# Batch 0's q heads in two PSUM banks, masks from one 64-column tile, batch 1 loaded pair by pair, tile 0 in two chunks

## The chip, the cores and the metric

The kernel runs on one core of a Trainium2 chip. A core has five engines that run side by side: TensorE (PE in the profile; its weight loads are PEld), VectorE (DVE), ScalarE (ACT), GpSimd (POOL) and SyncE (SP), each with its own in-order queue of instructions, and 16 DMA engines that they share. TensorE writes to PSUM, which has eight banks[...]. The metric is the device time of one execution in microseconds (us).

## The reference

Attention with a causal window of 64 positions over 8 batches, 8 heads, 576 positions and a head size of 64, and behind it an MLP with SiLU on its 4608 rows.

```python
scores = scale * np.matmul(q, k.transpose(0, 1, 3, 2))       # q, k, v: (8, 8, 576, 64) float32
rel = pos[:, None] - pos[None, :]
mask = (rel >= 0) & (rel < 64)
scores = np.where(mask, scores, -1e9)
attn = softmax(scores)                                       # over the last axis
x = (attn @ v).transpose(0, 2, 1, 3).reshape(4608, 512)
h = x @ w_in                                                 # (512, 2048)
out = (h * sigmoid(h)) @ w_out                               # (2048, 512), float32
```

## The kernel before

**Order.** The program is not written in its final order. Every piece of work is an operation in a list (`p.add(class, {engine: us}, function, deps, ...)`), and when the kernel is built a planner (`Plan.run`) plays the lists through: each engine takes, of the classes whose first operation is ready by the plan's clock, the one of the lowest rank, and the operations are issued in the order in which they were taken. The `us` of an operation, the `dma` of a load and the terms in `Plan.run` (line 98) are the plan's own cost numbers. They set the order on each in-order queue, and do not appear on the chip in any other way. An engine waits on the chip when its next instruction isn't ready, whatever stands behind it.

**Attention.** Heads are worked in pairs (four pairs `pj` per batch) and query rows in three groups `g` of 192. For each pair, q and k come in rows (`natb`), TensorE turns them (line 299, or line 309 in batch 0, where the load casts to bf16 on the way), and the turned blocks are lifted from PSUM to SBUF: `lift_q` (line 316) writes each head of the pair to its own half of the partitions of `qbd`, the other half of which is zero, and `lift_k` (line 322) writes `kt`. In batch 0 both heads of q are turned into one bank, and the two lifts read this bank. v is loaded into every second block of `vv`, and `shift_v` (lines 330 and 332) copies the halves that the overlapping key blocks need. Scores (line 344; 351 and 356 in batch 0), exponential (line 362), mask, values (line 370), reciprocal (line 376), norm, turning back (line 426; 415 in batch 0) and the copy into `bridge` (line 431) follow for each pair and group. From batch 2 on k, and later q and the outputs, are turned by DMA instead.

**Mask.** In batch 0, where TensorE has time, the mask is added to the scores: a matmul of the identity with `bias` or `bias0` (line 351) opens each score bank. From batch 1 on the exponentials are multiplied by `mask` or `mask0` (line 365). GpSimd builds `bias` and `mask` over six repeats of 64 columns each (lines 182 to 185), `bias` between the loads of pairs 1 and 2 of batch 0, `mask` behind the loads of pair 3; VectorE copies them to `bias0` and `mask0` and closes one block there.

**Loads.** GpSimd's queue carries, in this order: the identity; batch 0's q, k, v pair by pair (lines 241 and 269), with `bias` among them; `mask`; w_in in eight pieces (line 275); batch 1's q and k of all four pairs (line 234); two zero fills of `qbd` for batch 1 (line 218); batch 1's v (line 269); w_out in eight pieces (line 281); batch 2 and so on. `NIV` is the number of batches whose v is loaded pair by pair with q and k.

**MLP.** Rows go in nine tiles of 512. The first layer of a tile (line 435) runs over 16 blocks of 128 hidden units with 4 matmuls each, every block followed by a SiLU on ScalarE (line 441); the second layer (line 444) over 16 blocks for each of four row blocks, then a copy (line 450) and a store (line 454). `PARTS` cuts the columns of a first layer into chunks that can start when their rows of `bridge` are there: three for tile 0, two for tile 1. MLP matmuls have the rank behind all attention work, so they fill what attention leaves of TensorE; `scores_may_run` holds score matmuls back in the middle of a first layer. For the beginning there are up to 60 filler matmuls (line 668).

Of the kernel before, what the change touches and what calls it, by code (L numbers as in the profile page):

```python
# [9 lines left out]
BF16 = mybir.dt.bfloat16  # L10
ACTF = mybir.ActivationFunctionType
ALU = mybir.AluOpType


class Plan:
# [31 lines left out]
    def run(self):  # L47
# [7 lines left out]
        while left:  # L55
# [6 lines left out]
            while moved:  # L62
                moved = False
                for e in engines:
# [28 lines left out]
                    if op["dma"] is None:  # L93
                        op["seen"] = end + op["lat"]
                    else:

                        soft = e == "POOL"
                        pipe[soft] = max(pipe[soft], pipe[False], end + 0.6) + op["dma"]
                        op["seen"] = pipe[soft] + (2.0 if c in ("xk", "xo") else 1.4)
# [11 lines left out]
def kernel(ctx, tc, q, k, v, w_in, w_out, out):  # L111
# [16 lines left out]
    PARTS = {0: [(0, 192), (192, 384), (384, TT)], 1: [(0, 256), (256, TT)]}  # L128
    NXQ, NXK, NXO = 4, 2, 3
    NRAW, NOX = 2, 2  # L130
    NIV, NPM = 1, 1
# [10 lines left out]
    zero = keep.tile([128, NP], FP32, name="zero")  # L142
    mask0 = keep.tile([128, 3, 2, 64], BF16, name="mask0")
# [36 lines left out]
    def windows(t, fill, in_):  # L180
        m2 = t.rearrange("p t h i -> p (t h) i")
        nc.gpsimd.memset(m2, in_)
        nc.gpsimd.affine_select(out=m2, in_=m2, compare_op=ALU.is_ge, fill=fill,
                                base=-1, channel_multiplier=1, pattern=[[0, 6], [-1, 64]])
        nc.gpsimd.affine_select(out=m2, in_=m2, compare_op=ALU.is_ge, fill=fill,
                                base=64, channel_multiplier=-1, pattern=[[0, 6], [1, 64]])

    def const_bias(_):
        windows(bias, -30000.0, 0.0)

    def const_bias0(_):
        nc.vector.tensor_copy(out=bias0, in_=bias)
        nc.vector.memset(bias0[0:64, 0], -30000.0)

    def const_mask(_):
        windows(mask, 0.0, 1.0)

    def const_mask0(_):
        nc.vector.tensor_copy(out=mask0, in_=mask)
        nc.vector.memset(mask0[0:64, 0], 0.0)  # L200
# [29 lines left out]
    c_bias, c_mask = [], []  # L230
# [73 lines left out]
    def turn_heads(op, w):  # L304
        pst = at_bf16(op).rearrange("x (m p) -> x m p", m=NM)
        heads = natbs[w].rearrange("p m x -> p (m x)").rearrange("p (h m d) -> p h m d", h=2, m=NM)
        for m in range(NM):
            for hh in range(2):
                nc.tensor.matmul(  # L309
                    pst[64 * hh:64 * hh + 64, m], lhsT=heads[:, hh, m], rhs=ident[0:NR, 0:NR],  # L310
                    is_transpose=True, start=(m == 0), stop=(m == NM - 1),
                )
# [166 lines left out]
    def add_batch_qk(b):  # L479
        pool = "at" if b else "all"  # L480
        slot, parts = {}, {0: [], 1: []}
        for pj in range(NP):
            kq_done[(b, pj)] = []
            busy = s_last.get((b - NK, pj), []) + ([c_k[b % NK]] if b < NK else [])
            if (b, pj) == (0, 2):
                b1 = p.add("dma", {"POOL": 1.5}, const_bias)
                c_bias.append(p.add("one", {"DVE": 0.4}, const_bias0, [b1]))
            for kk in range(2):
# [29 lines left out]
                if b == 0:  # L518
                    ca = [p.add("dma", {"POOL": 0.66}, lambda _, w=w, pj=pj, kk=kk: load_cast(w, pj, kk), dma=0.87)]
                else:  # L520
                    i = n_nat[0] % NN
                    n_nat[0] += 1
                    cls, us = ("dma", {"POOL": 0.85}) if b in (1, 2) else ("ld0", {"SP": 0.45})
                    ld = p.add(cls, us, lambda e, i=i, pj=pj, kk=kk: load_qk(e, i, b, pj, kk),
                               [nat_free.get(i)] + (v_landed[b - 1] if b > 2 else []), dma=1.1)
                    ca = [p.add("cast", {"ACT": 0.84, "DVE": 0.56}, lambda e, i=i, w=w: cast(e, i, w),
                                [ld, natb_free.get(w)], b=b)]
                    nat_free[i] = ca[0]
                tu = p.add("turn", {"PE": 0.27 if b else 0.7}, None, ca + [c_ident] + busy, lat=0.1, pool=pool, b=b)
                tu["fn"] = lambda _, tu=tu, w=w: (turn if b else turn_heads)(tu, w)  # L530
                natb_free[w] = tu
                by = {"ACT": 0.64, "DVE": 0.75}
                if kk:
                    li = [p.add("lift", by, lambda e, tu=tu, pj=pj: lift_k(e, tu, b, pj), [tu] + busy, b=b)]
                else:
                    li = [p.add("lift", by, lambda e, tu=tu, pj=pj, hh=hh: lift_q(e, tu, b, pj, hh), [tu] + busy, b=b)
                          for hh in range(2)]
                tu["until"] = li
# [4 lines left out]
    def add_v_loads(b, parts, busy):  # L543
        v_landed.setdefault(b, []).extend(
            p.add("dma", {"POOL": 1.0}, lambda e, part=part: load_v(e, b, part), busy, dma=1.25) for part in parts)
# [117 lines left out]
    c_mask1 = p.add("dma", {"POOL": 1.5}, const_mask)  # L663
    c_mask.append(p.add("late", {"DVE": 0.4}, const_mask0, [c_mask1]))
# [8 lines left out]
    for f in range(8):  # L673
        win.append(p.add("dma", {"POOL": 0.8}, lambda _, f=f: load_w_in(f), dma=1.45))
    add_batch_attention(0)
    n_tile = 0
    for b in range(1, B):
# [4 lines left out]
        if b == 1:  # L682
            for f in range(8):
                wout.append(p.add("dma", {"POOL": 0.8}, lambda _, f=f: load_w_out(f), dma=1.45))
# [38 lines left out]
```

## Time and profile before

| | |
|---|---|
| median of 6 runs | 324.61 us (323.27 to 328.06) |
| the profiled execution, own time | 324.87 us |
| its span, first to last instruction | 323.1 us |
| mean granted TensorE clock | 0.989 |
| busy: PE, PEld | 305.2 us, 177.3 us |
| busy: ACT, DVE, POOL | 193.5, 165.4, 122.0 us |
| DMA moved | 39.41 MB in 135775 packets |

The profile is of one execution. Its rows by slices cut the span into 40 parts of 8.1 us and give tenths: a digit of 9 is 90% or more. The clock row gives what TensorE was granted of its full clock. In a timeline a row has the start, the duration, the engine, the line of the kernel, the operation, what is written and read, and in brackets how long the engine had been idle and what ended the wait. A matmul's own duration includes its latency, so for a stream of them the distance from start to start is used.

### The profile page before, as it was taken

The numbers are of one execution on the slowest core, as the hardware profiler recorded it, in microseconds if no ns is written. First come the engines' busy times: TensorE is split into PE (matmuls) and PEld (weight loads), VectorE is DVE, ScalarE is ACT, GpSimd is POOL, SyncE is SP. The second block draws the span as 40 slices with busy tenths as digits, with TensorE's granted clock in tenths as the row PEclk, the third lists the DMA queues.
The fourth block names the chain that finished last, engine by engine and source line by source line (L and its number), as shares of the span: only waits on it lengthen the run. The fifth ranks groups of instructions, "written<-read, shape, count | busy, mean of one in ns | idle before, by whom it ended". The sixth has DMA issues, their size and how long they took to land.

```text
span 323.1 us, 6251 instructions
## 1 busy us (share of the span) xinstructions
PE 305.2 (94%) x2289; PEld 177.3 (55%) x2314; DVE 165.4 (51%) x471; ACT 193.5 (60%) x392; POOL 122.0 (38%) x162
## 2 busy tenths in 40 slices
PE   1979979999999999999999999999999999999996
PEld 1657966668766555554554455445544444444444
DVE  3874796882888899893389178904810000000000
ACT  6658894688877757457835683568257226415611
POOL 8976966947272985875357000000000000000000
PEclk9979997999999999999999999999999999999999
DMA  8999999999999999999999983400430020021012
GB/s 89 137 166 244 200 199 222 164 129 276 151 158 157 168 150 155 179 139 200 144 175 182 160 127 91 114 3 0 117 89 0 34 81 16 0 85 46 1 56 76
DMA packets 135775, 39.41 MB, mean 122 GB/s; under 512 B 121664, under 2 KB 130496, under 8 KB 135744
## 3 DMA queue, kind: packets, MB, share of 16 engines
q0 software_dynamic: 93760, 19.54, 73.9%
q1 hardware_dynamic: 41984, 19.47, 31.9%
q8 instruction: 18, 0.29, 0.4%
q14 instruction: 13, 0.11, 0.1%
HBM read 36.70 MB, written 9.44 MB: 143 GB/s over the span
## 4 chain that ended last, share of the span: by engine, by line
PE 81%; DMA 8%; POOL 5%; DVE 3%; issue 1%; SPq 0%; ACT 0%; POOLq 0%; ACTq 0%
PE mp L444 38%; PE mp L435 32%; PE at L370 5%; PE at L344 5%; DMA nat<-in_k_dram 3%; DMA nat<-in_q_dram 3%; DMA w_in_sb<-in_moe_w_in_dram 3%; POOL natb L241 2%; POOL vv L269 1%; POOL w_in_sb L275 1%; PE at L299 1%; DVE qbd L316 1%; PE at L426 1%; DVE natb L288 1%; DVE ot L450 1%
## 5 line engine op out<-in xcount | busy, mean ns | idle before, releaser
L444 PE MATMUL mp<-w_out_sb,g 128*128 128x512 bf16 (+2 forms) x583 | 143.0, 369 | 1.1
L435 PE MATMUL mp<-bridge,w_in_sb 128*128 128x512 bf16 (+3 forms) x768 | 130.4, 326 | 0.4 <-ACT g L441 0.4
L441 ACT ACTIVATE g<-mp 128x512 bf16<-128x512 f32 (+3 forms) x192 | 91.2, 492 | 30.3 <-PE mp L435 29.0
L435 PEld LDWEIGHTS <-w_in_sb 128*128 128x128 bf16 x768 | 69.6, 98 | 52.1 <-issue 0.8
L444 PEld LDWEIGHTS <-g 128*128 128x128 bf16 x608 | 55.3, 98 | 43.1 <-issue 0.6
L450 ACT COPY ot<-mp 128x512 f32<-128x512 f32 (+2 forms) x33 | 18.5, 561 | 69.5 <-PE mp L444 61.4
L362 ACT ACTIVATE e<-at 128x384 bf16<-128x384 f32 x90 | 39.3, 497 | 7.1 <-PE at L344 5.8
L399 DVE TENSOR_TENSOR ox<-at,rc 64x192 bf16<-64x192 f32 x120 | 42.3, 353 | 2.4
L251 POOL DMA_DIRECT2D nat<-in_k_dram x48 | 35.0, 734 | 17.9 <-DMA vv<-in_v_dram 7.7
L365 DVE TENSOR_TENSOR e<-e,mask 128x384 bf16<-128x384 bf16 x84 | 26.3, 347 | 23.5 <-ACT e L362 22.8
L269 POOL DMA_DIRECT2D vv<-in_v_dram x32 | 32.7, 1025 | 14.2 <-PE at L370 9.6
L370 PE MATMUL at<-vv,e 128*128 128x130 bf16 x270 | 29.9, 221 | 4.0 <-DVE e L365 2.1
L370 PEld LDWEIGHTS <-e 128*128 128x128 bf16 x288 | 23.3, 98 | 18.5 <-DVE e L365 4.5
L251 POOL DMA_DIRECT2D nat<-in_q_dram x32 | 24.0, 756 | 13.5 <-DMA vv<-in_v_dram 9.0
L344 PE MATMUL at<-qbd,kt 128*128 128x128 bf16 x252 | 23.4, 220 | 0.2
L344 PEld LDWEIGHTS <-kt 128*128 128x128 bf16 x252 | 18.1, 98 | 8.4 <-issue 1.1
L376 DVE RECIPROCAL rc<-at 128x6 f32<-128x6 f32 x90 | 17.4, 195 | 9.2 <-PE at L370 7.2
L316 DVE COPY qbd<-at 64x576 bf16<-64x576 bf16 x22 | 16.6, 755 | 8.3 <-ACT qbd L316 4.3
L382 DVE TENSOR_TENSOR ob<-at,rc 64x192 bf16<-64x192 f32 x48 | 16.7, 349 | 0.9
L265 DVE COPY qbd<-raw 64x1152 bf16<-64x1152 bf16 x16 | 9.1, 570 | 8.8 <-DMA raw<-nat 8.4
L431 ACT CAST bridge<-at 128x192 bf16<-128x192 f32 x22 | 7.1, 323 | 6.0 <-PE at L426 4.6
L309 PE MATMUL at<-ident,natb 96*64 96x96 bf16 x72 | 3.4, 246 | 7.4 <-DMA natb<-in_q_dram 7.4
(70 smaller groups left out, 170.9 us busy)
## 6 DMA issues: line engine op xcount, KB each, us to landing
out_dram<-ot SPq DMA_DIRECT2D x35, 256.0 KB, 2.7
vv<-in_v_dram POOLq DMA_DIRECT2D x32, 144.0 KB, 7.8
nat<-in_k_dram POOLq DMA_DIRECT2D x48, 72.0 KB, 6.8
nat<-in_q_dram POOLq DMA_DIRECT2D x8, 288.0 KB, 9.6
nat<-in_q_dram POOLq DMA_DIRECT2D x32, 72.0 KB, 7.6
w_in_sb<-in_moe_w_in_dram POOLq DMA_DIRECT2D x8, 256.0 KB, 7.5
w_out_sb<-in_moe_w_out_dram POOLq DMA_DIRECT2D x8, 256.0 KB, 8.6
nat<-in_k_dram POOLq DMA_DIRECT2D x4, 288.0 KB, 10.3
```

The costliest lines, as they stand in the source:

```text
L251: nc.gpsimd.dma_start(out=rows(i)[:, pj % 2, :, 64 * hh:64 * hh + 64], in_=(q, k)[kk][b, 2 * pj + hh].rearrange("(m p) d -> p m d", p=NR),)
L269: queue[e].dma_start(out=vv[b % NK][:, 2 * g0 + 1:2 * g1 + 1:2, 0:D], in_=v[b].rearrange("h s d -> (h s) d").rearrange("(g p) d -> p g d", ...
L316: copies[e](out=qbd[b % NK][r, pj, hh].rearrange("x (p m) -> x p m", m=NM), in_=at_bf16(op)[r].rearrange("x (m p) -> x p m", m=NM),)
L344: nc.tensor.matmul(at_sp(op)[:, x], lhsT=kt[b % NK][:, pj * S + t * 64:pj * S + t * 64 + 128], rhs=qbd[b % NK][:, pj, :, t * 64:t * 64 + 6 ...
L362: nc.scalar.activation(out=es[n % NE], in_=at_sp(op), func=ACTF.Exp, scale=scale)
L365: nc.vector.tensor_mul(es[n % NE], es[n % NE], mask0 if g == 0 else mask)
L370: nc.tensor.matmul(at_pv(op)[:, x], lhsT=es[n % NE][:, x].rearrange("p h i -> p (h i)"), rhs=vv[b % NK][:, s:s + NB + 1:NB, 0:D + 1], star ...
L399: nc.vector.tensor_mul(ox(n)[:, :, r], pv[r, :, hh, 0:D], rc[r, :, hh:hh + 1].to_broadcast([64, 3, 64]))
L435: nc.tensor.matmul(banks[bank["bank"]][:, lo:hi], lhsT=w_in_sb[:, c, ft * 128:(ft + 1) * 128], rhs=bridge[:, (j * TT + lo) // 64:(j * TT + ...
L441: nc.scalar.activation(out=gts[gt][:, lo:hi], in_=banks[bank["bank"]][:, lo:hi], func=ACTF.Silu)
L444: nc.tensor.matmul(banks[bank["bank"]][:, 0:hi - lo], lhsT=gts[gt][:, m * 128:(m + 1) * 128], rhs=w_out_sb[:, f, lo:hi], start=(f == 0), s ...
L450: copies[e](out=ots[ot][:, lo:hi], in_=banks[bank["bank"]][:, 0:hi - lo])
```

## The change

The identity's tile is followed on GpSimd by a `window` tile of 64 columns (a memset and two selects), ahead of all loads; VectorE spreads it into `bias` and `bias0` with broadcast copies, and later computes `mask` and `mask0` from these with a multiply and an add (-32768 becomes 0, 0 becomes 1). The two places in GpSimd's queue where `bias` and `mask` were built are gone. In batch 0, the heads of a q pair are turned as two operations, each with a bank and one lift of its own. `NIV` is 2, so batch 1 is loaded as q, k, v of each pair in turn, and its zero fills come behind these loads. Tile 0 has two chunks instead of three, tile 1 one instead of two. In the plan, a second lift from the same bank now waits for the first, and the cost numbers of the loads are changed. These numbers and the new dependencies can change the planned order throughout.

```diff
-                        pipe[soft] = max(pipe[soft], pipe[False], end + 0.6) + op["dma"]
+                        pipe[soft] = max(pipe[soft], pipe[False], end + 0.9) + op["dma"]
...
-    PARTS = {0: [(0, 192), (192, 384), (384, TT)], 1: [(0, 256), (256, TT)]}
+    PARTS = {0: [(0, 192), (192, TT)]}
...
-    NIV, NPM = 1, 1
+    NIV, NPM = 2, 1
...
+    window = keep.tile([128, 64], BF16, name="window")
...
-    def windows(t, fill, in_):
-        m2 = t.rearrange("p t h i -> p (t h) i")
-        nc.gpsimd.memset(m2, in_)
-        nc.gpsimd.affine_select(out=m2, in_=m2, compare_op=ALU.is_ge, fill=fill,
-                                base=-1, channel_multiplier=1, pattern=[[0, 6], [-1, 64]])
-        nc.gpsimd.affine_select(out=m2, in_=m2, compare_op=ALU.is_ge, fill=fill,
-                                base=64, channel_multiplier=-1, pattern=[[0, 6], [1, 64]])
+    def const_window(_):
+
+        nc.gpsimd.memset(window, 0.0)
+        nc.gpsimd.affine_select(out=window, in_=window, compare_op=ALU.is_ge, fill=-32768.0,
+                                base=-1, channel_multiplier=1, pattern=[[-1, 64]])
+        nc.gpsimd.affine_select(out=window, in_=window, compare_op=ALU.is_ge, fill=-32768.0,
+                                base=64, channel_multiplier=-1, pattern=[[1, 64]])
 
     def const_bias(_):
-        windows(bias, -30000.0, 0.0)
-
-    def const_bias0(_):
-        nc.vector.tensor_copy(out=bias0, in_=bias)
-        nc.vector.memset(bias0[0:64, 0], -30000.0)
+        for t in (bias, bias0):
+            nc.vector.tensor_copy(out=t.rearrange("p t h i -> p (t h) i"),
+                                  in_=window.unsqueeze(1).to_broadcast([128, 6, 64]))
+        nc.vector.memset(bias0[0:64, 0], -32768.0)
 
     def const_mask(_):
-        windows(mask, 0.0, 1.0)
-
-    def const_mask0(_):
-        nc.vector.tensor_copy(out=mask0, in_=mask)
-        nc.vector.memset(mask0[0:64, 0], 0.0)
+        for a, m in ((bias, mask), (bias0, mask0)):
+            nc.vector.tensor_scalar(m, a, 1.0 / 32768.0, 1.0, op0=ALU.mult, op1=ALU.add)
...
-    c_bias, c_mask = [], []
+    c_window = p.add("one", {"POOL": 0.6}, const_window)
+    c_bias = [p.add("one", {"DVE": 0.9}, const_bias, [c_window])]
+    c_mask = [p.add("late", {"DVE": 0.7}, const_mask, c_bias)]
...
-    def turn_heads(op, w):
+    def turn_heads(op, w, hs):
         pst = at_bf16(op).rearrange("x (m p) -> x m p", m=NM)
         heads = natbs[w].rearrange("p m x -> p (m x)").rearrange("p (h m d) -> p h m d", h=2, m=NM)
         for m in range(NM):
-            for hh in range(2):
+            for hh in hs:
...
-            if (b, pj) == (0, 2):
-                b1 = p.add("dma", {"POOL": 1.5}, const_bias)
-                c_bias.append(p.add("one", {"DVE": 0.4}, const_bias0, [b1]))
...
-                    ca = [p.add("dma", {"POOL": 0.66}, lambda _, w=w, pj=pj, kk=kk: load_cast(w, pj, kk), dma=0.87)]
+                    ca = [p.add("dma", {"POOL": 0.66}, lambda _, w=w, pj=pj, kk=kk: load_cast(w, pj, kk), dma=1.0)]
...
-                tu = p.add("turn", {"PE": 0.27 if b else 0.7}, None, ca + [c_ident] + busy, lat=0.1, pool=pool, b=b)
-                tu["fn"] = lambda _, tu=tu, w=w: (turn if b else turn_heads)(tu, w)
+                by = {"ACT": 0.64, "DVE": 0.75}
+                li = []
+
+                for hs in ([(0,), (1,)] if b == 0 and not kk else [(0, 1)]):
+                    us = 0.27 if b else 0.35 * len(hs)
+                    tu = p.add("turn", {"PE": us}, None, ca + [c_ident] + busy, lat=0.1, pool=pool, b=b)
+                    tu["fn"] = lambda _, tu=tu, w=w, hs=hs: turn(tu, w) if b else turn_heads(tu, w, hs)
+                    if kk:
+                        tu["until"] = [p.add("lift", by, lambda e, tu=tu, pj=pj: lift_k(e, tu, b, pj), [tu] + busy, b=b)]
+                    else:
+                        for hh in hs:
+                            tu["until"].append(p.add("lift", by, lambda e, tu=tu, pj=pj, hh=hh: lift_q(e, tu, b, pj, hh),
+                                                     [tu] + busy + tu["until"], b=b))
+                    li += tu["until"]
                 natb_free[w] = tu
...
-    c_mask1 = p.add("dma", {"POOL": 1.5}, const_mask)
-    c_mask.append(p.add("late", {"DVE": 0.4}, const_mask0, [c_mask1]))
```

Left out of the diff are the other changed cost numbers of loads: batch 1's q and k 1.1 to 1.15, v 1.25 to 1.3, w_in 1.45 to 1.55, w_out 1.45 to 1.38.

More of the change, by code (lines that the diff above doesn't have):

```diff
@@ L524, in add_batch_qk @@
                     ld = p.add(cls, us, lambda e, i=i, pj=pj, kk=kk: load_qk(e, i, b, pj, kk),
[L525 removed]
+                               [nat_free.get(i)] + (v_landed[b - 1] if b > 2 else []), dma=1.15)
                     ca = [p.add("cast", {"ACT": 0.84, "DVE": 0.56}, lambda e, i=i, w=w: cast(e, i, w),
@@ L528, in add_batch_qk @@
                     nat_free[i] = ca[0]
-                tu = p.add("turn", {"PE": 0.27 if b else 0.7}, None, ca + [c_ident] + busy, lat=0.1, pool=pool, b=b)
-                tu["fn"] = lambda _, tu=tu, w=w: (turn if b else turn_heads)(tu, w)
-                natb_free[w] = tu
[L532 to L538, printed above, removed]
+                by = {"ACT": 0.64, "DVE": 0.75}
[11 more added lines that the diff above has]
+                    li += tu["until"]
+                natb_free[w] = tu
                 kq_done[(b, pj)] += li
@@ L544, in add_v_loads @@
         v_landed.setdefault(b, []).extend(
-            p.add("dma", {"POOL": 1.0}, lambda e, part=part: load_v(e, b, part), busy, dma=1.25) for part in parts)
+            p.add("dma", {"POOL": 1.0}, lambda e, part=part: load_v(e, b, part), busy, dma=1.3) for part in parts)
     def add_batch_v(b):
@@ L673 @@
     for f in range(8):
-        win.append(p.add("dma", {"POOL": 0.8}, lambda _, f=f: load_w_in(f), dma=1.45))
+        win.append(p.add("dma", {"POOL": 0.8}, lambda _, f=f: load_w_in(f), dma=1.55))
     add_batch_attention(0)
@@ L683 @@
             for f in range(8):
-                wout.append(p.add("dma", {"POOL": 0.8}, lambda _, f=f: load_w_out(f), dma=1.45))
+                wout.append(p.add("dma", {"POOL": 0.8}, lambda _, f=f: load_w_out(f), dma=1.38))
         while TB * (n_tile + 1) <= b * NB:
```

## The prediction, made before the changed kernel was run

> **What bounds the kernel now.** I read the engine rows first, then the chain of work that ended last, then the landings of the DMAs, then the timelines of the two places where TensorE stands still.
>
> ```profile
> PE 305.2 (94%) x2289; PEld 177.3 (55%) x2314; DVE 165.4 (51%) x471; ACT 193.5 (60%) x392; POOL 122.0 (38%) x162
> PE   1979979999999999999999999999999999999996
> PEclk9979997999999999999999999999999999999999
> ```
>
> TensorE bounds the kernel from slice 7 on (a slice is 8.1 us). Everything that can still be won lies in the first 50 us and in the two dips of the clock row (slices 2 and 6). Behind them VectorE is done at 240 us and TensorE has only matmuls left, so a microsecond that tile 1 starts earlier is a microsecond of the end.
>
> ```profile
> 14.23 3.67 POOL w_in_sb L275 x5
> 17.90 8.38 DMA w_in_sb<-in_moe_w_in_dram
> 26.56 9.07 DMA nat<-in_k_dram
> 35.65 1.49 DVE natb L288 x2
> ```
>
> The chain runs through GpSimd's issues to 17.90, then through DMA to 35.65. The completion times in the trace say how tight that is: batch 0's twelve loads land from 4.81 (q of pair 0) to 17.17 (v of pair 3), one per 1.12 us; w_in from 19.16 to 29.18, one per 1.43; batch 1's q and k from 30.87 to 39.29 and its v to 42.91; w_out from 44.16 to 53.18, one per 1.29. The DMA row shows no hole between 3.3 and 53 us.
>
> ```profile
> 17.52 0.75 DVE L316 COPY qbd<-at 64x576 bf16<-64x576 bf16 x1
> 18.30 0.64 ACT L316 COPY qbd<-at 64x576 bf16<-64x576 bf16 x1 [1.57 <-DVE qbd L316]
> 18.96 0.49 ACT L362 ACTIVATE e<-at 128x384 bf16<-128x384 f32 x1
> 19.50 0.51 PE L370 MATMUL at<-vv,e 128*128 128x130 bf16 x3 [1.75 <-ACT e L362]
> ```
>
> And the same stretches in the table by windows (start:end, length, busy PE, PEld, DVE, ACT, POOL, clock, DMA share, GB/s):
>
> ```profile
> 20.00:25.00 5.00, 5.00 (x52) 3.80 (x50) 2.97 (x11) 3.35 (x10) 2.77 (x5) 0.73 1.39 182
> 45.00:50.00 5.00, 2.09 (x19) 1.16 (x19) 4.68 (x14) 3.14 (x5) 2.98 (x5) 1.00 1.24 206
> 50.00:55.00 5.00, 5.00 (x41) 3.14 (x40) 2.97 (x10) 2.53 (x7) 2.95 (x5) 0.66 1.51 230
> ```
>
> Stand-still one, in the timeline: ScalarE's half of a q pair waits 1.57 us for VectorE's half, because both read one bank; the exponential behind it is late, and TensorE waits 1.75 us and then runs at half clock. Stand-still two: of the 5 us from 45 TensorE works 2.09, while VectorE works 4.68. It is behind with batch 1's casts, lifts and eight v shifts; the mask runs at 48.59, though ScalarE began that score group at 46.19. The clock falls again (0.66).
>
> **Part by part.**
>
> *The window tile goes ahead of the first load.* A GpSimd select took 0.29 us on 128 columns and 0.54 on 384, a memset 0.20 and 0.44: a straight line gives 0.23 and 0.14 for 64. Two selects, a memset and three gaps of 0.07 come to 0.81 us, and every load of batch 0 is issued that much later. It removes 1.6 us of GpSimd before pair 2 (6.31 to 7.91) and 1.6 before w_in (12.53 to 14.18). I credit the first with nothing: q of pair 2 landed 0.72 us after the load ahead of it, so the DMA side was just in step, and the pace of 1.12 us holds before and after that hole. So q of pair 0 lands at 5.6, k of pair 3 at 17.05 instead of 16.25. If the deeper queue does speed the stream up, pair 3 lands at 15.5, the issue bound. I keep 17.05. The second hole is worth 0.6: the first w_in came 1.99 us after the last v, the others 1.43 apart. From w_in on the stream is therefore 0.2 us late: w_out begins at 44.4.
>
> *The masks on VectorE.* Two copies (0.26), a memset (0.17), and later two multiply-adds (about 0.26 each) replace a copy and memset of each kind (0.43 and 0.36): 0.4 us more of VectorE in all, the first part in idle time at 2 to 3 us. A rule speaks against it. The Trainium skill (SBUF — State Buffer, "Who interferes with whom") says that a VectorE copy in a two-port mode and GpSimd lock each other out for a whole instruction, and these copies run while GpSimd writes the first descriptors. The row: v shifts, copies within SBUF too, took 0.60 to 0.82 us beside GpSimd's issues instead of 0.32, while an issue beside such copies took 0.79 instead of 0.68. By the rule the first loads could wait both copies, 0.5 us; by the row 0.1. I take 0.1, which the w_in gap swallows.
>
> *Two banks for q.* The same 12 transposes, but head 0 is lifted while head 1 is turned, and neither engine waits for the other. VectorE waited for ScalarE's half 3.8 us in three places, ScalarE for VectorE's 1.6. Pair 0: q at 5.6, head 0 turned 0.35 later, lifted by 6.6; k at 6.4, turned by 7.1, lifted (0.64) by 7.8. The bias is long there, where it came only at 9.25. First scores at 7.9 instead of 9.46. Pair 3: k at 17.05, turn 0.45, lift 0.76: its scores begin at 18.3 instead of 21.08, since neither wait of stand-still one is left. From these scores to tile 0 it took 6.1 us (21.08 to 27.19): tile 0 starts near 24.4. Bank pressure: one more of eight for half a microsecond, nothing.
>
> *Tile 0 in two chunks, tile 1 in one.* Start to start a matmul of 128, 192, 256 and 512 columns takes 58, 83, 111 and 216 ns, so 320 takes 137. Tile 0's first layer: 64 x (83+83+58) = 14.3 us becomes 14.1. Tile 1: 128 x 111 = 14.2 becomes 13.8, 0.4 us less. Waiting for all of batch 0 costs nothing, its groups end together; for tile 1 see the rivals.
>
> *Tile 0's early start is mostly taken back.* At 24.4 the w_in pieces just keep ahead (the last lands at 29.4; TensorE asks at 28.9: 0.5 lost). The first layer ended 17.2 us after its start with six turns inside; now at about 41. The second layer cannot start before w_out lands, 44.4. So 2.8 us of start become 46.09 - 44.4 = 1.7.
>
> *Batch 1 pair by pair.* Same loads, but v of pair 0 lands at about 33.3 instead of 40.3, so the shifts (0.32 each) move into VectorE's idle stretch (30 to 35: 1.60 of 5 busy), and k of pair 3 lands at 42.1 instead of 39.3. That costs nothing while k waits anyway: its cast ran at 47.32. The two zero fills (2.46 us) move behind v on GpSimd, ahead of w_out: that is issued near 37.8, and landings of 7.4 us after issue hold 3 us of queue, so it still comes at 44.4. Stand-still two, 2.1 us (46.9 to 49.0), goes, because the three score groups that now run after 41 have 3 us without second-layer work.
>
> *The half clock.* TensorE then has little to do for some 3 us before 44.4. The Trainium skill (TensorE: Matmul & The Clock Gate, "HAM oscillation — how this bites in real kernels") puts the limit at idle gaps over about 3.4 us: scores in between would keep the clock, and 1.5 us more would be won. The rows are stricter: gaps of 1.75 and 2.1 us each brought about 3 us at 0.50 (from 19.3 and 50.0), losing 1.5. I leave the 1.5 lost.
>
> **The sum.** From the turn at 45.83 to tile 1's start at 69.97 TensorE has 64 x 0.216 = 13.8 us of second layer, 9 score groups x 0.17, 12 value groups x 0.17, 12 x 0.09 back, and six turns x 0.26: 20.0. Begun at 44.4, less 0.4 of turns done before, plus 1.5 half clock and 0.5 small waits: 66.0, so 4.0 gained. With tile 1's 0.4: 4.4. The profiled execution took 324.87 (span 323.1 and 1.8 around it), 0.3 over the median of 324.61. 324.87 - 4.4 = **320.5**.
>
> **Rivals.**
> *A, the start is won and then lost in batch 1.* VectorE does some 3.6 us per pair (a cast, two lifts, k's lift, two shifts) against a landing pace of 3.2, and it stood idle from 31.6 to 34.07 because a turn sat behind MoE matmuls in TensorE's order. If that stays, its backlog ends near 48 as before, stand-still two grows by the 1.7 won: only tile 1's 0.4 is left, 324.4. For it: VectorE at 4.8 of 5 from 35 to 50. Against: ScalarE is freed of 16 silus after 41.
> *B, pair 3 of batch 1 becomes the wait: slower.* The scores go group by group over all pairs, so every group needs pair 3, and tile 1 in one piece needs the last group. k is 2.8 us later, and VectorE, the bound in A, adds 1.6 of lag. The last bridge moves from about 68.3 to 72.7; tile 1 starts 2.7 later, the idle from 66 on costs 1.7 of clock: 324.87 + 2.7 + 1.7 - 0.4 = 328.9. It decides from the point where the last bridge is later than 70.4. Against it: 8 us of slack on k's cast.
> *That batch 0 gains nothing* (the 0.8 is all that is left) leads to A's number, since w_out sets the next start.
>
> **How the numbers follow.** Forecast 0.62, own range 317.5 to 322.5 (without the half clock 319.0, and with the deeper queue's 1.5 us 317.5); A 0.20; B 0.18. A measurement of this kernel tells about 1% from no change, 3.2 us: faster begins at 321.4. Nine tenths of the forecast lie below that: 0.57 faster; B's upper three quarters and a little more are slower, 0.16; the rest 0.27. The range reaches through A into B: 317.0 to 327.5.
>
> **What would show it.** First scores before 8.5; ScalarE's wait for VectorE's lift gone; tile 0 at 23.5 to 25.5; w_out from 44 to 45; second layer within 0.5 us of it; no 2 us gap after 46; tile 1 near 66. Wrong if pair 3 of batch 0 lands after 18.5, w_out after 46, or the last bridge of batch 1 after 70.

## The result, and the profile after

The changed kernel takes 323.18 us (median of 35 runs), the kernel before 325.63 (72 runs); the ratio is 0.9935, with a 95% interval of 0.9918 to 0.9952. So 2.1 us were won, where 4.4 had been forecast (320.5 us). A second measurement gave 0.9929 (0.9895 to 0.9963). Medians are over all executions, while ratios leave out those more than 1.5% above the fastest of their kernel, so the two can differ (1.6% by medians and 0.9% by the ratio for three and two chunks below).

The profiled execution took 325.59 us (span 323.7), more than the median. From its page, the busy times and the rows by slices:

```profile
PE 310.0 (96%) x2182; PEld 169.5 (52%) x2207; DVE 158.4 (49%) x465; ACT 192.6 (59%) x371; POOL 120.3 (37%) x159
PE   5999778999999999999999999999999999999996
PEclk9999987999999999999999999999999999999999
```

Slices are counted from 0. The dip of the clock in slice 2 is gone; slices 4 and 5 have TensorE at 7, and slices 5 and 6 have a lower clock. The loss has moved from batch 0 to tile 0's first layer. The timeline of VectorE in that place (start, duration, engine, line, operation; in brackets the idle time before it and what ended that):

```profile
32.99 0.75 DVE L315 COPY qbd<-at 64x576 bf16<-64x576 bf16 x1 [2.67 <-PE at L298]
36.49 0.76 DVE L315 COPY qbd<-at 64x576 bf16<-64x576 bf16 x1 [2.75 <-POOL qbd L215]
37.27 0.76 DVE L321 COPY kt<-at 128x576 bf16<-128x576 bf16 x1
38.04 0.34 DVE L331 COPY vv<-vv 64x576 bf16<-64x576 bf16 x1
38.39 0.32 DVE L329 COPY vv<-vv 64x576 bf16<-64x576 bf16 x1
38.75 0.59 DVE L287 CAST natb<-nat 96x768 bf16<-96x768 f32 x1
```

and of TensorE:

```profile
34.13 2.61 PE L434 MATMUL mp<-bridge,w_in_sb 128*128 128x320 bf16 x18
...
36.84 0.44 PE L434 MATMUL mp<-bridge,w_in_sb 128*128 128x320 bf16 x2
39.40 0.65 PE L298 MATMUL at<-ident,natb 96*128 96x96 bf16 x6 [2.12 <-DVE natb L287]
39.84 4.09 PE L434 MATMUL mp<-bridge,w_in_sb 128*128 128x320 bf16 x18
```

The second lift of pair 0 of batch 1 waits 2.75 us for GpSimd's zero fill of the same tile (line 215 here). Behind it in VectorE's queue stand a k lift, two shifts and a cast; the turn of the block that is cast stands in TensorE's queue ahead of first-layer matmuls, and TensorE stops for 2.1 us. Then 18 matmuls of 320 columns take 4.09 us, where 18 took 2.61 before the stop. The table by windows (columns as in the prediction; the clock is the third number from the end) has the granted clock at half there:

```profile
41.00:42.00 1.00, 1.00 (x6) 0.52 (x5) 0.94 (x3) 0.37 (x2) 0.77 (x2) 0.50 1.66 168
```

GpSimd's queue shows why the fill is so late:

```profile
26.30 1.03 POOL L268 DMA_DIRECT2D vv<-in_v_dram  x1 [1.88 <-DMA w_in_sb<-in_moe_w_in_dram]
...
35.41 2.16 POOL L215 MEMSET qbd<- 64x1152 f32 x2
```

Before each of batch 1's twelve loads GpSimd stood idle until an earlier load had landed, 8.2 us in all (the first line is the longest of these waits). The plan has no such waits: by its clock the fills are done at 30.3 us, before the first lift at 31.6. On the chip they are done at 37.6.

Milestones of several kernels (one execution each; first instruction of each kind, us; the clock is the mean of the execution; "changed, second profile" is the same kernel profiled again):

| | before | forecast | changed | changed, second profile | fills early | fills early, fillers late | NIV 1 |
|---|---|---|---|---|---|---|---|
| first scores | 9.46 | 7.9 | 9.89 | 10.08 | 9.89 | 7.05 | 9.11 |
| tile 0, first layer | 27.19 | 24.4 | 25.20 | 25.24 | 26.30 | 25.53 | 24.46 |
| tile 0, second layer | 46.09 | 44.4 | 50.02 | 48.11 | 47.69 | 46.10 | 46.22 |
| tile 1, first layer | 69.97 | 66.0 | 70.99 | 68.55 | 68.08 | 66.90 | 65.14 |
| span | 323.1 | | 323.7 | 320.6 | 320.2 | 319.1 | 317.3 |
| clock | 0.989 | | 0.988 | 0.993 | 0.993 | 0.994 | 1.000 |

Tile 0 starts 2.0 us earlier (2.8 were forecast). Its second layer, forecast 1.7 earlier, starts 2 to 4 us later. Tile 1 starts between 1.4 earlier and 1.0 later. Ahead of the second layer TensorE still works for only 2.67 of 5 us (2.09 before; its busy time is the first number after the length):

```profile
45.00:50.00 5.00, 2.67 (x35) 1.85 (x32) 4.82 (x11) 4.19 (x8) 2.87 (x4) 0.97 1.24 204
```

### The profile page after: what moved, and what is told of

Same layout as the page of the kernel before. It is cut to its first block, busy times and chain, and to the rows that moved or that the text cites. A ratio compares the mean times of both kernels' runs of the same rounds, so it can differ in the third digit from the quotient of the medians.

```text
span 323.7 us, 6015 instructions
## 1 busy us (share of the span) xinstructions
PE 310.0 (96%) x2182; PEld 169.5 (52%) x2207; DVE 158.4 (49%) x465; ACT 192.6 (59%) x371; POOL 120.3 (37%) x159
## 4 chain that ended last, share of the span: by engine, by line
PE 80%; DMA 9%; POOL 5%; DVE 3%; issue 2%; ACT 1%; SPq 1%; POOLq 0%; ACTq 0%
PE mp L443 37%; PE mp L434 32%; DMA nat<-in_q_dram 6%; PE at L369 5%; PE at L343 5%; DMA w_in_sb<-in_moe_w_in_dram 3%; POOL natb L240 2%; POOL vv L268 2%; PE at L298 1%; DVE qbd L315 1%; PE at L425 1%; POOL w_in_sb L274 1%; DVE natb L287 1%; DVE kt L321 0%; ACT qbd L315 0%
## 5 line engine op out<-in xcount | busy, mean ns | idle before, releaser
L434 PE MATMUL mp<-bridge,w_in_sb 128*128 128x512 bf16 (+2 forms) x640 | 130.8, 361 | 0.0
L440 ACT ACTIVATE g<-mp 128x512 bf16<-128x512 f32 (+2 forms) x160 | 86.5, 556 | 31.8 <-PE mp L434 30.5
L434 PEld LDWEIGHTS <-w_in_sb 128*128 128x128 bf16 x640 | 61.1, 99 | 60.0 <-issue 0.2
L443 PEld LDWEIGHTS <-g 128*128 128x128 bf16 x608 | 54.6, 98 | 41.3 <-issue 0.3
L250 POOL DMA_DIRECT2D nat<-in_k_dram x48 | 36.0, 755 | 26.7 <-DMA nat<-in_k_dram 11.6
L369 PEld LDWEIGHTS <-e 128*128 128x128 bf16 x288 | 22.2, 97 | 15.7 <-DVE e L364 4.3
L343 PE MATMUL at<-qbd,kt 128*128 128x128 bf16 x252 | 24.1, 222 | 0.9 <-DVE kt L321 0.5
L315 DVE COPY qbd<-at 64x576 bf16<-64x576 bf16 x13 | 9.7, 749 | 12.2 <-PE at L308 4.8
L315 ACT COPY qbd<-at 64x576 bf16<-64x576 bf16 x16 | 10.2, 635 | 8.3 <-DVE qbd L315 3.7
L287 DVE CAST natb<-nat 96x768 bf16<-96x768 f32 x11 | 6.3, 593 | 13.8 <-DMA nat<-in_q_dram 13.5
```

What stands on the lines that cost most here:

```text
L250: nc.gpsimd.dma_start(out=rows(i)[:, pj % 2, :, 64 * hh:64 * hh + 64], in_=(q, k)[kk][b, 2 * pj + hh].rearrange("(m p) d -> p m d", p=NR),)
L315: copies[e](out=qbd[b % NK][r, pj, hh].rearrange("x (p m) -> x p m", m=NM), in_=at_bf16(op)[r].rearrange("x (m p) -> x p m", m=NM),)
L343: nc.tensor.matmul(at_sp(op)[:, x], lhsT=kt[b % NK][:, pj * S + t * 64:pj * S + t * 64 + 128], rhs=qbd[b % NK][:, pj, :, t * 64:t * 64 + 6 ...
L369: nc.tensor.matmul(at_pv(op)[:, x], lhsT=es[n % NE][:, x].rearrange("p h i -> p (h i)"), rhs=vv[b % NK][:, s:s + NB + 1:NB, 0:D + 1], star ...
L434: nc.tensor.matmul(banks[bank["bank"]][:, lo:hi], lhsT=w_in_sb[:, c, ft * 128:(ft + 1) * 128], rhs=bridge[:, (j * TT + lo) // 64:(j * TT + ...
L440: nc.scalar.activation(out=gts[gt][:, lo:hi], in_=banks[bank["bank"]][:, lo:hi], func=ACTF.Silu)
```

## The experiments

All ratios are to the kernel before, measured together with it, with 95% intervals.

### The zero fills

*Fills ahead of batch 1's loads* (the queues of TensorE, VectorE and ScalarE keep their order):

```diff
     for b in range(1, B):
-        add_batch_qk(b)
         if b == 1:
             c_q[1] = [p.add("dma", {"POOL": 1.3}, lambda e, hh=hh: clear_q(e, 1, hh)) for hh in range(2)]
+        add_batch_qk(b)
         add_batch_v(b)
```

> The changed kernel with batch 1's two zero fills of qbd issued on GpSimd right behind w_in, ahead of batch 1's loads, instead of behind them; every other queue keeps its order. Theory 1 (the fill is the wait): VectorE's second lift of batch 1 no longer waits 2.75 us for GpSimd, the 2.1 us stand-still of TensorE at 37.3 and the half clock behind it (1.6 us) go, the second layer begins near 46.5 instead of 50.0, and the time falls by 2.5 to 4 us against the changed kernel, to 319.5 to 320.5 (ratio to before 0.982 to 0.985). Theory 2 (VectorE's work is the bound in batch 1): the wait only took slack; the lift starts earlier and the next cast or lift waits instead, less than 1 us is won (ratio 0.990 to 0.994).

Measured: 321.62 us, 0.9887 (0.9854 to 0.9920), 0.004 to 0.005 below the changed kernel, some 1.4 us, between the two theories (the two intervals just touch). VectorE and TensorE in its timeline:

```profile
34.08 1.52 DVE L315 COPY qbd<-at 64x576 bf16<-64x576 bf16 x2 [4.54 <-PE at L298]
```

```profile
38.20 0.42 PE L298 MATMUL at<-ident,natb 96*128 96x96 bf16 x6
38.46 2.61 PE L434 MATMUL mp<-bridge,w_in_sb 128*128 128x320 bf16 x18
```

Both lifts run without a gap between them, the turn without a wait, and the 18 matmuls at full clock: the stand-still and its half clock are gone, as theory 1 has it. But three later waits of TensorE stay (0.6, 1.0 and 0.6 us, for k's lift, a cast and a mask), and with them a later half-clock stretch (0.66 from 45 to 50 us), so the second layer starts at 47.69, not 46.5.

*The kernel before with its fills behind batch 1's v*, the same move backwards; here too the other three queues keep their order:

```diff
     for b in range(1, B):
         add_batch_qk(b)
+        add_batch_v(b)
         if b == 1:
             c_q[1] = [...]
-        add_batch_v(b)
```

> The kernel before with only the two zero fills moved behind batch 1's v loads on GpSimd. Theory 1: batch 1's first lift on VectorE, at 34.07, now waits until the fills end near 36.8, TensorE's turn or mask behind it waits as long, and with a half-clock stretch the time rises by 2 to 4 us (ratio 1.006 to 1.012). Theory 2: VectorE had 2.5 us of idle time there, so less than 1 us is lost (ratio 0.999 to 1.003).

Measured: 332.45 us, 1.0221 (1.0166 to 1.0275), nearly twice the upper expectation. In the kernel before, both lifts run without a gap and wait for a turn only:

```profile
34.07 1.54 DVE L316 COPY qbd<-at 64x576 bf16<-64x576 bf16 x2 [2.47 <-PE at L299]
```

With the late fills:

```profile
38.21 0.76 DVE L316 COPY qbd<-at 64x576 bf16<-64x576 bf16 x1 [4.13 <-POOL qbd L218]
```

```profile
39.75 0.66 PE L299 MATMUL at<-ident,natb 96*128 96x96 bf16 x6 [4.23 <-DVE natb L288]
```

The lift waits 4.13 us, TensorE 4.23, and tile 1 starts at 75.55 instead of 69.97. So the place of two memsets in GpSimd's queue is worth 7 us in the kernel before. The fill and the lift touch no common element: a fill writes one head's columns in one half of the partitions, the lift that waits writes the other head's columns there. The built program holds the lift back all the same; the wait is in VectorE's row. In the changed kernel the pair's first lift did not wait, though both fills stand ahead of it in the program: its columns lie in front of the first column of the other fill, while the second lift's lie between the first and last columns of the fill it waits for. That fits a wait set by the range that a fill spans and not by its elements; no run tested it.

*The fills left behind v, but the plan told of the wait*:

```diff
             c_q[1] = [...]
+            for x in range(NP):
+                for op in kq_done[(1, x)][:2]:
+                    op["deps"] += c_q[1]
```

> The changed kernel with the fills where they are, but with the plan told that batch 1's q lifts wait for them. Theory 1 (the loss is that the plan does not know of the wait): VectorE gets k lifts, shifts and casts ahead of the q lifts, TensorE's 2 us stand-still near 38 shrinks below 1, 0.984 to 0.990. Rival (the fills are late, known or not, and every q of batch 1 comes later): 0.992 to 0.998.

Measured: 323.59 us, 0.9937 (0.9913 to 0.9960), a number that fits the rival. But the edit changed nothing: by the plan's clock the fills are done at 30.3 us and the first of these lifts starts at 31.6, so the new dependency is met in any case, and every queue has the order of the changed kernel. Theory 1 was not tested; the run is a third measurement of the changed kernel (VectorE waits 2.53 us for the fill). What the plan lacks is GpSimd's waits, which make the fills 7 us later than it has them. Whether a plan with the right times would avoid the loss stays open.

### The fillers

```diff
-    p.add_filler(60, "warm", ..., gate=lambda: moe[40][0]["seen"] is None,
+    p.add_filler(60, "warm", ..., gate=lambda: exps.get(0) and exps[0][0]["seen"] is not None and moe[40][0]["seen"] is None,
```

> The changed kernel with filler matmuls allowed only after the first exponential has been planned. Theory 1 (the fillers at half clock sit ahead of pair 0's turns): q of pair 0 is turned when it lands, 4.7, not at 6.51, k at 6.4, not 8.69, first scores near 8 instead of 9.89; tile 0 begins 0.5 to 1.3 us earlier than 25.79, but the end moves by less than 0.7 us because batch 1's VectorE chain sets it (ratio 0.991 to 0.994). Rival: the fillers bring the full clock early; without them the first pairs run at half clock, tile 0 starts no earlier and the time is 0 to 1 us longer than the changed kernel's (0.9935 to 0.997).

Measured: 321.90 us, 0.9898 (0.9856 to 0.9939). In the changed kernel `bias`, which the fillers read, is there at 3.5 us, and fillers stand in the queue ahead of the turns of pair 0, whose q landed at 4.64 and k at 6.36:

```profile
3.54 1.44 PE L667 MATMUL at<-bias,ident 128*128 128x384 bf16 x4 [3.54 <-DVE bias L191]
...
4.77 1.48 PE L667 MATMUL mp<-bias,ident 128*128 128x384 bf16 x4
6.05 0.52 PE L667 MATMUL at<-bias,ident 128*128 128x384 bf16 x1
6.51 0.86 PE L308 MATMUL at<-ident,natb 96*64 96x96 bf16 x12
...
8.69 0.45 PE L308 MATMUL mp<-ident,natb 96*64 96x96 bf16 x12
```

A filler there comes every 0.32 us (from 9.4 us on every 0.16); the plan gives it 0.17. Without them the scores begin at 7.11:

```profile
7.11 0.50 PE L350 MATMUL at<-bias,ident 128*128 128x384 bf16 x1
```

That is 2.8 us earlier, yet tile 0 starts at 25.34, no earlier than with them (25.20, 25.24). So theory 1 is right on the scores and wrong on tile 0. The ratio is lower by 0.003 to 0.004 all the same, though the intervals overlap: in the profiled execution the first layer took 17.5 us instead of 20.2 and 17.8, the second layer starts at 46.71, and the clock is 0.999. The order differs by more than the fillers: with them gone from the start, the plan's queues of TensorE, VectorE and ScalarE change up to some 65 us of the plan's clock. Which of these changes shortens batch 1 was not followed further.

*Both*: fills early and fillers late.

> Both: zero fills behind w_in and fillers only after the first exponential. Theory 1 of both: the earlier tile 0 can now count, 319 to 320 (ratio 0.980 to 0.984), bounded by w_out, whose first piece lands near 43.6. Theory 2: as the changed kernel, 0.990 to 0.995.

Measured: 320.18 us, 0.9839 (0.9800 to 0.9878). Within the intervals the two gains add. This version beats both kernels.

### One part undone at a time

*Batch 1's loads*, all of q and then all of k again, the rest as changed; the fills then stand between k and v:

```diff
-    NIV, NPM = 2, 1
+    NIV, NPM = 1, 1
```

> The changed kernel with NIV back at 1: batch 1's q and k of all pairs first, then the zero fills, then its v. Theory 1 (loading pair by pair put the fills late and cost what it won): VectorE's lift no longer waits for a fill, the stand-still at 37.3 goes as with the fills moved early, but v of pair 0 lands near 39.5 and its shifts fall into VectorE's full stretch, so about 1 us is lost again: 0.988 to 0.994. Rival (pair by pair is what won): the stand-still of 45 to 49 of the kernel before returns in full, 0.995 to 1.000.

Measured: 320.85 us, 0.9860 (0.9815 to 0.9904), faster than the changed kernel by 0.0075 and below theory 1's range. TensorE does not stand still, neither at 37 nor at 46 us (its longest wait from 10 to 90 us is 0.9), and the second layer starts at 46.22. Loading pair by pair, with the fills that move along with it, costs 2.4 us here. Some 1.4 of them are the fills' (fills early); the other 1.0 lies within the intervals of the two runs. It wins nothing that shows. Together with late fillers:

> The changed kernel with NIV back at 1 and fillers only after the first exponential. If the two effects add (0.0075 and 0.004 below the changed kernel): 0.980 to 0.984, near 319.5. If w_out, whose first piece lands near 43, or batch 1's casts bound both: as with either alone, 0.985 to 0.989.

Measured: 320.56 us, 0.9848 (0.9796 to 0.9900): at the edge between the two cases, no surer than either alone.

*One bank* in batch 0:

```diff
-                for hs in ([(0,), (1,)] if b == 0 and not kk else [(0, 1)]):
+                for hs in [(0, 1)]:
```

> The changed kernel with both heads of batch 0's q pairs turned into one bank again, the second lift waiting for the first. Theory 1 (two banks only shorten batch 0): tile 0 starts 0.5 to 1.5 us later than in the changed kernel, and the end moves by less than 0.7 us, because batch 1's VectorE chain and w_out set the second layer: 0.992 to 0.997. Rival (batch 0's wait between the lifts is the core of the gain): ScalarE waits for VectorE's lift again, TensorE falls to half clock in batch 0 and 2 us are lost: 0.998 to 1.002.

Measured: 324.58 us, 0.9956 (0.9921 to 0.9991). Two banks are worth about 0.002, 0.7 us, and the interval overlaps the changed kernel's. Tile 0 starts no later with one bank (25.01), and batch 0's stand-still of TensorE does not come back: from 10 to 39 us TensorE waits nowhere for as long as 0.55 us, and up to 30 us ScalarE never waits for VectorE's lift. That this stand-still is gone is therefore not shown to be the work of the two banks. The plan's new dependency between two lifts of one bank, which this version keeps, is a candidate; it was not tested alone.

*Three and two chunks*:

```diff
-    PARTS = {0: [(0, 192), (192, TT)]}
+    PARTS = {0: [(0, 192), (192, 384), (384, TT)], 1: [(0, 256), (256, TT)]}
```

> The changed kernel with tile 0 in three chunks and tile 1 in two again. Theory 1 (only matmul count): tile 1's first layer costs 128 x 111 ns instead of 64 x 216, 0.4 us, tile 0's 0.2 more: 0.994 to 0.997. Rival (the shorter, more frequent SiLUs burden ScalarE just when it is to cast and lift for batch 1): tile 0's and tile 1's first layers are longer by 1 us and more each: 0.998 to 1.003.

Measured: 330.85 us, 1.0089 (1.0039 to 1.0139). The chunks were forecast at 0.6 us and are worth 5.0. To tell ScalarE's share from TensorE's, the SiLUs alone were cut:

```diff
-                si.append(p.add("silu", {"ACT": 0.18 + (hi - lo) * 0.00083}, lambda ...: silu(bank, g, lo, hi), ...
+                cut = {0: [384], 1: [256]}.get(j, [])
+                ends = [lo, *[x for x in cut if lo < x < hi], hi]
+                si.append(p.add("silu", {"ACT": 0.18 * (len(ends) - 1) + (hi - lo) * 0.00083},
+                                lambda ...: [silu(bank, g, x, y) for x, y in zip(ends, ends[1:])], ...
```

> The changed kernel with its two chunks and one chunk of matmuls, but the SiLU of a block cut where the three and two chunks of before cut it: tile 0's second chunk in 192 and 128 columns, tile 1's in 256 and 256. So ScalarE has the many short SiLUs of before and TensorE the few long matmuls. Theory 1 (the chunks cost through ScalarE: 16 more SiLUs in tile 0 and 16 in tile 1, some 0.15 to 0.2 us each, leave casts and lifts of batches 1 to 3 to VectorE): close to the three-and-two-chunk version, 1.002 to 1.010. Theory 2 (through TensorE: more matmuls, and other places for the turns among them): as the changed kernel, 0.991 to 0.996.

Measured: 325.76 us, 0.9973 (0.9941 to 1.0006), between both. ScalarE's many short SiLUs make about 1.2 of the 5.0 us (the intervals overlap); 0.6 is the matmuls' count, by the prediction's sum. The other 3 were not separated; the planned order changes with the chunks, from 31 us of the plan's clock on.

*Masks on GpSimd again* (the functions and places of the kernel before):

```diff
-    c_window = p.add("one", {"POOL": 0.6}, const_window)
-    c_bias = [p.add("one", {"DVE": 0.9}, const_bias, [c_window])]
-    c_mask = [p.add("late", {"DVE": 0.7}, const_mask, c_bias)]
...
+        windows(bias, -30000.0, 0.0)
...
+        windows(mask, 0.0, 1.0)
```

> The changed kernel with bias and mask built on GpSimd between the loads again. Theory 1 (DMA paces the loads, not GpSimd's issue): k of pair 0 lands 0.7 us earlier, pair 3 and w_in at most 0.7 us later, bias comes near 9.3 so first scores near 9.5; no fillers ahead of the first turns; time within 0.7 us of the changed kernel: 0.991 to 0.996. Rival (the freed GpSimd time is the gain): pair 3 and w_in are 1 to 2 us later, tile 0 starts that much later and 1.5 to 2 us are lost: 0.997 to 1.001.

Measured: 327.88 us, 1.0068 (1.0036 to 1.0100): slower than either case. The trace's completions show why the rival is nearer: the last w_in piece lands at 30.39 instead of 28.77 and the first w_out at 45.87 instead of 43.58, and VectorE's wait for the fill is 4.63 us. So the freed GpSimd time is worth about 2 us of the DMA stream, and a later stream makes the fills later still. The planned order differs too, so not all of the 4.3 us need be the stream's.

### The plan's cost numbers

*The changed kernel with the six old numbers* (0.6, 0.87, 1.1, 1.25, 1.45, 1.45), of which the first two are:

```diff
-                        pipe[soft] = max(pipe[soft], pipe[False], end + 0.9) + op["dma"]
+                        pipe[soft] = max(pipe[soft], pipe[False], end + 0.6) + op["dma"]
...
-                    ca = [..., load_cast(w, pj, kk), dma=1.0)]
+                    ca = [..., load_cast(w, pj, kk), dma=0.87)]
```

> The changed kernel with the plan's old cost numbers for loads. Theory 1 (the numbers move turns ahead of their data): turns of batches 0 and 1 stand earlier in TensorE's queue than their data lands, waits of TensorE for casts grow by 1 to 3 us, 0.996 to 1.005. Rival (the numbers matter little, since the waits come from the zero fills and VectorE): 0.991 to 0.996.

Measured: 335.16 us, 1.0296 (1.0257 to 1.0335). The structural parts without the numbers are 3% slower than the kernel before. Who waited for whom, up to 90 us (total, times, longest):

```profile
PE at L298 <- DVE natb L287: 8.0, 3, 5.2
...
DVE qbd L315 <- POOL qbd L215: 4.8, 1, 4.8
```

and far behind, in the timeline:

```profile
196.61 0.45 DVE L264 COPY qbd<-raw 64x1152 bf16<-64x1152 bf16 x1 [9.86 <-DMA raw<-nat]
...
199.52 0.34 PE L369 MATMUL at<-vv,e 128*128 128x130 bf16 x3 [4.82 <-DVE e L364]
```

One loss is the fill's wait, 4.8 us instead of 2.75. The other is in batch 7: VectorE waits for a DMA transpose of q, the masks behind it are late, and TensorE, whose queue has value matmuls there, stops for 4.8 us.

*The same with the fills early*, *the kernel before with the new numbers alone*, and *the changed kernel with the two old numbers of the start* (0.6 and 0.87):

> The changed kernel with the old numbers and the zero fills right behind w_in. Theory 1 (with the old numbers the lift is put before the fill is done, 4.8 us of wait on VectorE and 5.2 on TensorE): the loss at 34 to 40 us goes, 3 to 5 us; the 4.8 us that TensorE waits for a mask near 200 us stays: 1.010 to 1.020. Rival (the old numbers put the turns ahead of the data whatever the fills do): less than 1.5 us won, 1.025 to 1.030.

> The kernel before with only the plan's new cost numbers for loads. Theory 1 (the new numbers fit the landings of this chip and help any version): TensorE's waits for casts and masks between 30 and 72 us (3.2 us) shrink, 0.985 to 0.993. Theory 2 (the numbers only repair what the other parts of the change break): 0.997 to 1.006.

> The changed kernel with two of the six old numbers, the 0.6 us from issue to transfer and 0.87 us per load of batch 0; v, batch 1, w_in and w_out keep the new ones. Theory 1 (these two start the plan's DMA clock and shift all that follows): most of the loss, 1.010 to 1.030. Theory 2 (the sum over w_in and batch 1 is what matters): close to the changed kernel, 0.992 to 1.000.

Measured: 1.0101 (1.0054 to 1.0147), 328.63 us; 1.0181 (1.0129 to 1.0233), 332.02 us; 1.0052 (1.0022 to 1.0083), 328.82 us. The first is as theory 1 has it: 2% came through the fills, and TensorE's wait for a mask in batch 7 stays. The second is against both theories: the new numbers alone make the kernel before slower by 1.8%, and TensorE has the same wait:

```profile
195.40 0.51 PE L370 MATMUL at<-vv,e 128*128 128x130 bf16 x3 [5.29 <-DVE e L365]
```

```profile
193.86 0.51 PE L369 MATMUL at<-vv,e 128*128 128x130 bf16 x3 [5.96 <-DVE e L364]
```

(the kernel before with new numbers, then the changed kernel with old numbers and early fills). What VectorE had waited for in the first of the two is not the transpose but v:

```profile
193.43 0.75 DVE L332 COPY vv<-vv 64x2304 bf16<-64x2304 bf16 x1 [5.80 <-DMA vv<-in_v_dram]
```

So the numbers are not better in themselves; numbers and structure have to match, or the order of batch 7 is off by 5 us. The two start numbers carry about a third of the loss (0.0117 of 0.0361); no single number was found to carry it.

*The changed kernel again*:

> The changed kernel itself again, beside the others on one chip, with a second profile. Theory 1: VectorE's lift waits 2 to 3 us for the zero fill again, and the ratio is 0.991 to 0.996; what differs between its executions is the number of half-clock stretches, 1.7 us each. Rival: the wait was an accident of one execution and is gone in this one.

Measured: 0.9929, as above. The lift waited 1.54 us in this execution, just below the 2 to 3 of theory 1, and the span is 320.6 with one half-clock stretch before 80 us instead of two. TensorE at the same place, here and in the run that told the plan of the fills:

```profile
38.22 0.43 PE L298 MATMUL at<-ident,natb 96*128 96x96 bf16 x6 [0.91 <-DVE natb L287]
38.49 2.61 PE L434 MATMUL mp<-bridge,w_in_sb 128*128 128x320 bf16 x18
```

```profile
39.58 0.43 PE L298 MATMUL at<-ident,natb 96*128 96x96 bf16 x6 [1.89 <-DVE natb L287]
39.85 4.28 PE L434 MATMUL mp<-bridge,w_in_sb 128*128 128x320 bf16 x18
```

With the first profile these are three executions of one program: behind stops of 1.89 and 2.12 us the clock fell to half, behind one of 0.91 it did not. The wait for the fill is no accident; its length varies, and with it whether the clock falls.

## Why the prediction was right or wrong

The direction was right, for a part of the reasons. The size was twice too large. The step that failed first is the one on the zero fills in "Batch 1 pair by pair": it put the second layer at 44.4 us, and it came at 48.1 to 50.2. By the prediction's steps:

- **"The two zero fills ... it still comes at 44.4".** w_out did come, at 43.58. But the fills were priced for what stands behind them on GpSimd and not for who waits for them, VectorE's lifts. That cost was put at nothing. The runs show a wait of 1.5 to 2.75 us on VectorE, a stop of 0.9 to 2.1 us on TensorE and, behind the longer stops, half clock. Taking it away wins some 1.4 of the 2.3 us that are missing. The outcome is rival A's, a start that is won and lost again in batch 1 (323.18 us lies between the forecast and A's 324.4). A's idle stretch of VectorE is there too (2.67 us before the first lift), but the 1.4 us come by a wait for the fills, which A did not have. What makes up the rest of the 2.3 us stays open.
- **w_out as the bound of the second layer.** It was not the bound in any profile: second layers began 1.9 to 7.9 us after its first piece had landed.
- **Pair by pair** was to win the 2.1 us of stand-still two and costs 2.4, fills included. v of pair 0 landed at 32.35 (forecast 33.3), but its shifts did not move into VectorE's idle stretch: they stand behind the waiting lift and run at 38.04. Stand-still two did not go: of the 5 us from 45 TensorE works 2.67 (2.09 before). In the version without pair by pair (NIV 1) it works 4.48 of them.
- **Window tile.** Its length was right (0.80 us, forecast 0.81), its place was not: the change puts it "ahead of all loads", and it runs behind the first, q of pair 0, because in its class's list it stands behind VectorE's clears. q landed at 4.64 (forecast 5.6), k of pair 0 at 6.36 (forecast 6.4). "I credit the first with nothing" failed: k of pair 3 landed at 15.67, not 17.05, close to the 15.5 that the prediction gave for a stream that the deeper queue speeds up. With the masks back on GpSimd the w_out stream is 2.3 us later. The pace of 1.12 us per load was not a limit of DMA alone.
- **The rule on ports** was weighed rightly by the row: the two issues beside the copies took 0.65 and 1.03 us, where k and v issues of batch 0 took 0.63 to 0.65 and 1.01 to 1.03 in the kernel before.
- **Two banks.** Stand-still one is gone, as said, but it is gone with one bank too. The first scores were not at 7.9 but at 9.89: the early bias lets fillers in ahead of the turns. That the fillers read `bias` was in the code and not considered. Tile 0 came at 25.2 instead of 24.4.
- **Chunks.** The count of matmuls was right, the step mis-sized: 0.6 us forecast, 5.0 measured, about 1.2 of it through ScalarE.
- **Half clock.** Leaving 1.5 us in was right. A stop of 2.1 us brought about 3.4 us at 0.50 (39.4 to 42.9 us), as gaps of 1.75 and 2.1 had before the change. The Trainium skill (TensorE: Matmul & The Clock Gate, "HAM oscillation — how this bites in real kernels") puts the limit at about 3.4 us of idle time, by which none of these stops would have cost anything; the measurement decides. Where no stop passed 0.93 us (NIV 1) the clock is 1.000.
- **What was not in the sum at all:** the plan's cost numbers. They were named in the change as able to reorder everything, and priced at zero without a reason. Set back alone they cost 3.6%, more than any other part.
- **The sum itself** added the parts as if each had its own price. Undone one at a time, two banks, chunks, masks and cost numbers are worth 0.7, 5.0, 4.3 and 11.7 us and pair by pair -2.4, some 19 us together, while the whole change wins 2.1. The price of a part holds only with the others in place, because each edit gives a new planned order.

The version with early fills and late fillers (320.18) nearly meets the forecast time. That does not make the steps right: tile 0 and the second layer come later in it than forecast, and NIV 1 reaches 320.85 without either edit, so a number near 320.5 does not tell which parts made it.

## What to carry to other kernels

When a step moves an instruction in one queue, look for everyone who reads or writes the same tile, not only for what stands behind it in that queue; here two memsets of some 1.1 us each, moved by four loads, decided up to 7 us. A plan's clock is to be compared with the trace before it is trusted: this one had the fills done 7 us earlier than the chip, so telling it of a dependency changed nothing. An operation that becomes ready earlier also sets free whatever was waiting for it, fillers too, and on an in-order queue these go ahead of the real work. Where an order is planned with cost numbers, a change of the numbers is a part of the change with its own price, and has to be tried together with the structure: alone, the old numbers on the new kernel and the new numbers on the old one were both slower.

## What the runs showed of the hardware

Stops of TensorE of 1.89 and 2.12 us were followed by about 3.4 us at half clock, a stop of 0.91 us in the same program was not. The length of one stop is not all of it: in all three profiles of that program another half-clock stretch began between 46.7 and 50.2 us, behind several stops of at most 1.22 us each; in the first profile TensorE was busy for 0.36 of the 2 us from 46. Executions of one kernel differ by this: the changed kernel's first two profiles lost 3.4 and 1.7 us to half clock before 80 us, 1.7 of the 3.1 us between their spans (323.7 and 320.6). DMA transposes that SyncE issued between 177 and 191 us, behind each other, landed 6.7 to 9.7 us after their issue in the changed kernel with old numbers, and one issued alone at 204 landed after 3.2. There VectorE stood idle for 9.86 us, so a queue that counts on such a transpose has to be planned that far ahead.
